# Strided attention products one place sooner, and one local mask moved behind two normalisations, in a fused attention and MLP kernel

## The chip, the cores and the metric

The kernel runs on one core of a Trainium2 chip. The metric is the device time of one execution in microseconds (us); lower is better. A core has five engines that run their own instruction streams side by side and wait for one another by semaphores: TensorE (PE, matrix products and transposes, results in PSUM), VectorE (DVE), ScalarE (ACT), GpSimd (POOL) and SyncE (SP, which starts transfers). Each engine takes its instructions in the order in which the program emits them, so in this kernel, whose schedule is written by hand, the place of a line in a list decides what an engine does first.

## The reference

Sparse attention over 8 images of 576 tokens with 8 heads of 64, and an MLP with a Mish activation behind it.

```python
def _attn_ref(q, k, v):                      # (8, 8, 576, 64) each
    scores = (1 / sqrt(D)) * q @ k.transpose(0, 1, 3, 2)
    rel = pos[:, None] - pos[None, :]
    mask_local   = (rel >= 0) & (rel < 32)                       # heads 0..3
    mask_strided = (rel >= 0) & (pos[None, :] % 32 == pos[:, None] % 32)   # heads 4..7
    attn = softmax(where(mask, scores, -1e9))
    return attn @ v

def _moe_ref(x, w_in, w_out):                # x (4608, 512): tokens x (heads, dim)
    h = x @ w_in                             # (4608, 2048)
    g = h * tanh(softplus(h))                # Mish
    return g @ w_out                         # (4608, 512)
```

## The kernel before

The 4608 tokens are cut into nine blocks of 512. Stage t of the main loop does the MLP of block t: first MLP1 (`w_in`, then Mish on ACT), then MLP2 (`w_out`). Both are lists of small groups of matmuls. Between the groups, stage t also computes the attention of image t + 1, one step of a list at each place, so that PE always has matmuls of the MLP to do while other engines work on the attention.

The main loop, cut. `g1` are the groups of MLP1, `a1` the steps put between them; `at` are the steps put between the groups of MLP2. For t = 3 to 6 the lists are `str_steps` and `loc_steps`:

```python
for t in range(NBLK):
    x, y, z = accs
    # ... (stages 0 to 2 use other lists)
    elif t + 1 < B:
        a1 = str_steps(t + 1)
        at = loc_steps(t + 1, x, y)
    # ...
    for i, g in enumerate(g1):
        g()
        if i < len(a1):
            for s in a1[i]:
                s()
    # ... casts and loads for later images
    for i, g in enumerate(mlp2(t, gT, out_accs, fc_major=(t == 0))):
        g()
        if i < len(at):
            for s in at[i]:
                s()
```

A group of MLP2 is four matmuls of 512 columns. The first six groups of MLP1 are four matmuls each, too, and so are the ten behind them (more and shorter ones where a block wraps around the end of its buffer, as in t = 4).

The two lists that the change touches:

```python
def str_steps(b):
    a = Attn(b)
    V = lambda i: (lambda: a.pv("s", i))
    return [
        [], [], [V(0)], [V(1)], [V(2)], [V(3)], [V(4)], [V(5)], [V(6)], [V(7), a.xt_str],
    ]

def loc_steps(b, x, y):
    a = Attn(b)
    Q = lambda i_acc, *parts: (lambda: a.qk(parts, i_acc))      # scores on PE, exp on ACT
    M = lambda kd, i: (lambda: a.mask(kd, i, nc.vector))
    V = lambda i: (lambda: a.pv("l", i))
    more = b + 1 < B
    n2 = (("n", 2),) if more else ()
    N = [lambda i=i: a.mask("n", i, nc.gpsimd) for i in range(3)]
    return [
        [],
        [Q(x, ("l", 0)), Q(None, ("l", 2), *n2), Q(y, ("l", 1)), M("l", 0), M("l", 2)],
        [], [],
        [V(0), V(1), M("l", 1)],
        [V(5)] + ([Q(x, ("n", 0)), Q(y, ("n", 1))] + N) * more + [a.xt_str_copy],
        [V(2)],
        [V(3)],
        [V(4), lambda: a.xt_loc(0, NW)],
        [], [], [], [], [], [], [],
    ]
```

"s" is strided, "l" local, "n" the strided scores of the next image. The local probabilities of six query tiles lie in three buffers: part 0 serves tiles 0 and 1 (and half of 2), part 1 the rest of 2, and 3 and 4, part 2 tile 5. A mask multiplies one such part by zeros and ones; a `pv` step multiplies the masked probabilities by v on PE and divides by the sum on DVE:

```python
def mask(self, kind, i, meng):
    # pm: a part of the probabilities, two halves x tiles x columns; mk: the mask, broadcast
    meng.tensor_tensor(out=pm, in0=pm, in1=mk..., op=ALU.mult)

def pv(self, kind, i):
    po = tile_t("po")...                     # one of two PSUM buffers
    self.pv_mm(kind, i, po)                  # four products on PE
    nc.vector.reciprocal(rden[0:m, :], po[0:m, :, D])
    nc.vector.tensor_tensor(out=dst..., in0=po[0:m, :, 0:D], in1=rden..., op=ALU.mult)

def xt_str(self):                            # twelve transposes on DVE, behind V(7)
    for q in range(4):
        for m in range(0, 96, 32):
            nc.vector.transpose(xs_t[32*q:32*q+32, :, :, m:m+32], src[m:m+32, :, :, q, :])

def xt_str_copy(self):                       # their result into the MLP's input, on ACT
    for c in range(2):
        nc.scalar.copy(...)
```

Of the kernel before, what the change touches and what calls it, by code (L numbers as in the profile page):

```python
# [38 lines left out]
def kernel(ctx, tc, q, k, v, moe_w_in, moe_w_out, out):  # L39
# [368 lines left out]
    def str_steps(b):  # L408

        a = Attn(b)  # L410
        V = lambda i: (lambda: a.pv("s", i))
        return [
            [], [], [V(0)], [V(1)], [V(2)], [V(3)], [V(4)], [V(5)], [V(6)], [V(7), a.xt_str],
        ]

    def loc_steps(b, x, y):

        a = Attn(b)
        Q = lambda i_acc, *parts: (lambda: a.qk(parts, i_acc))
# [4 lines that stand above are left out]
        N = [lambda i=i: a.mask("n", i, nc.gpsimd) for i in range(3)]  # L424
        return [
            [],
            [Q(x, ("l", 0)), Q(None, ("l", 2), *n2), Q(y, ("l", 1)), M("l", 0), M("l", 2)],
            [], [],
            [V(0), V(1), M("l", 1)],
            [V(5)] + ([Q(x, ("n", 0)), Q(y, ("n", 1))] + N) * more + [a.xt_str_copy],  # L430
            [V(2)],
            [V(3)],
            [V(4), lambda: a.xt_loc(0, NW)],
            [], [], [], [], [], [], [],
        ]
# [131 lines left out]
    with tc.manual_schedule():  # L567
# [35 lines left out]
        a = Attn(0)  # L603
# [69 lines left out]
        for t in range(NBLK):  # L673
            x, y, z = accs
# [3 lines left out]
            if t == 0:  # L678
                ts, at = t_steps(1), attn_steps(1, y, y)
                at[0] = ts[2:4] + [cast_v1]  # L680
                at[9] += [lambda: str_by_dma(2), lambda: loc_by_dma(2)]
                out_accs, accs = (z, x), (y, z, x)
            else:
                if t <= 2:
                    at = attn_steps(t + 1, x, y, z if t == 2 else None)
# [3 lines that stand above are left out]
                if t == 1:  # L689
                    at[9].append(lambda: str_by_dma(3))  # L690
                if t == 2:
                    Dv.memset(x_s[64:96], 0.0)
                if t + 2 < B:
                    at[9].append(lambda: loc_by_dma(t + 2))
                if 1 < t < B - 3:
                    at[9].append(lambda: str_by_dma(t + 3))
                out_accs, accs = (z, y), (z, x, y)
# [61 lines left out]
```

The softmax here doesn't subtract the row's maximum and nothing guards it: scores larger than these inputs give would overflow.

## Time and profile before

| | |
|---|---|
| time, median of 3 runs | 314.95 us (314.67 to 316.58) |
| profiled span | 312.8 us, 5771 instructions |
| PE busy | 295.3 us (94%) |
| ACT busy | 182.6 us (58%) |
| DVE busy | 164.6 us (53%) |
| POOL busy | 102.4 us (33%) |

Times inside the profile are counted from the start of the span. A line of the timeline gives the start, the length, the engine, the line of the program, the operation, the operands with their shapes, the number of instructions merged into the line, and in brackets how long the engine stood idle before it and what ended that. The chain that ended last is followed back from the last instruction; its shares tell which engine the end of the kernel hangs on. A table of windows gives, for each stretch, its length and then the busy time of each engine with its number of instructions, the granted clock of PE, the busy share of the DMA engines, and GB/s. PE's ends are modelled, so its starts are the safer numbers.

### The profile page before, as it was taken

How to read it: one execution, taken by the hardware profiler on the slowest of the kernel's cores; microseconds unless marked ns; L12 is line 12 of the kernel's file. 1: busy time of each engine (PE TensorE's matmuls, PEld its weight loads, DVE VectorE, ACT ScalarE, POOL GpSimd, SP SyncE). 2: the span in 40 equal slices, each digit the busy share in tenths (PEclk: the TensorE clock that was granted, in tenths of full speed). 3: DMA queues.
4: the chain of work that ended last, by engine and by line, in shares of the span. 5: the costliest groups of instructions: out<-in, count | busy, mean ns of one | idle time of the engine just before them, and what ended most of it. 6: DMA issues, size and time to landing. Idle time of an engine off the chain costs nothing.

```text
span 312.8 us, 5771 instructions
## 1 busy us (share of the span) xinstructions
PE 295.3 (94%) x2376; PEld 156.2 (50%) x2376; DVE 164.6 (53%) x378; ACT 182.6 (58%) x195; POOL 102.4 (33%) x109
## 2 busy tenths in 40 slices
PE   0687999999999999999999999999999999999995
PEld 0563455544454445554469754545454444444444
DVE  7673066700571048569786988698869870000000
ACT  1673653476647673867786778677767937215501
POOL 9199043263046105230791079108800000000000
PEclk9999999999999999999999999999999999999999
DMA  6999999999999999999987999898330030011011
GB/s 174 203 226 206 221 185 199 176 168 130 222 188 207 126 221 187 197 165 211 188 162 127 208 169 185 146 198 159 103 107 2 0 132 4 0 67 69 0 67 67
DMA packets 96985, 45.14 MB, mean 144 GB/s; under 512 B 79040, under 2 KB 89600, under 8 KB 96960
## 3 DMA queue, kind: packets, MB, share of 16 engines
q1 hardware_dynamic: 85520, 35.66, 61.8%
q0 software_dynamic: 11152, 8.92, 18.8%
q8 instruction: 18, 0.29, 0.4%
q10 hardware_dynamic: 288, 0.21, 0.2%
q14 instruction: 7, 0.06, 0.1%
HBM read 36.78 MB, written 9.44 MB: 148 GB/s over the span
## 4 chain that ended last, share of the span: by engine, by line
PE 85%; DVE 11%; ACT 2%; issue 1%; DVEq 0%
PE psh L507 38%; PE pso L530 31%; PE po L323 5%; PE pso L557 4%; PE ps L286 3%; DVE xs_t L397 3%; DVE Pl L307 2%; DVE ks L149 1%; DVE x_l L335 1%; PE trx L362 1%; PE tr L209 1%; DVE x_s L335 1%; PE trx L372 1%; DVE rden L334 1%; DVE Ps L601 0%
## 5 line engine op out<-in xcount | busy, mean ns | idle before, releaser
L507 PE MATMUL psh<-xT,w_in 128*128 128x512 bf16 (+1 forms) x640 | 131.9, 361 | 0.3 <-ACT Ps L299 0.3
L530 PE MATMUL pso<-w_out,gT 128*128 128x512 bf16 x512 | 121.8, 379 | 0.0
L513 ACT ACTIVATE gT<-psh 128x1024 bf16<-128x1024 f32 x72 | 72.4, 1023 | 50.1 <-PE psh L507 50.1
L507 PEld LDWEIGHTS <-w_in 128*128 128x128 bf16 x640 | 60.5, 98 | 57.1 <-issue 2.5
L530 PEld LDWEIGHTS <-gT 128*128 128x128 bf16 x512 | 45.4, 98 | 45.8
L149 POOL CAST kl<-kl 96x768 bf16<-96x768 f32 (+1 forms) x13 | 12.5, 984 | 78.8 <-DMA kl<-in_k_dram 78.8
L397 DVE STREAM_TRANSPOSE xs_t<-x_s 32x512 bf16<-32x512 bf16 x48 | 33.7, 702 | 0.9
L334 DVE RECIPROCAL rden<-po 72x4 f32<-72x4 f32 (+1 forms) x100 | 17.6, 176 | 28.1 <-PE po L323 27.2
L537 ACT COPY osb<-pso 128x1024 f32<-128x1024 f32 x16 | 17.6, 1100 | 24.3 <-PE pso L530 13.9
L307 DVE TENSOR_TENSOR Ps<-Ps,consts_sb 72x864 bf16<-72x864 bf16 (+3 forms) x15 | 10.2, 688 | 38.6 <-ACT Ps L299 38.6
L149 DVE COPY osb<-pso 128x512 f32<-128x512 f32 (+1 forms) x2 | 1.1, 558 | 51.3 <-PE pso L557 51.3
L388 DVE STREAM_TRANSPOSE xT<-x_l 32x384 bf16<-32x384 bf16 x48 | 27.3, 569 | 0.7
L149 POOL CAST vl<-vl 128x768 bf16<-128x768 f32 (+2 forms) x30 | 23.6, 785 | 9.0 <-DMA vl<-in_v_dram 7.6
L299 ACT ACTIVATE Ps<-ps 72x864 bf16<-72x864 f32 (+3 forms) x21 | 17.4, 860 | 13.4 <-PE ps L286 13.4
L335 DVE TENSOR_TENSOR x_s<-po,rden 72x256 bf16<-72x256 f32 x56 | 23.5, 420 | 1.9
L323 PEld LDWEIGHTS <-Ps 72*128 72x128 bf16 x256 | 15.5, 101 | 12.0 <-DVE Ps L307 0.8
L404 ACT COPY xT<-xs_t 128x576 bf16<-128x576 bf16 x8 | 21.4, 2938 | 0.0
L299 ACT ACTIVATE Pl<-ps 128x960 bf16<-128x960 f32 (+1 forms) x20 | 17.3, 874 | 3.7 <-PE ps L286 3.5
L335 DVE TENSOR_TENSOR x_l<-po,rden 96x256 bf16<-96x256 f32 x44 | 18.5, 421 | 1.5
L323 PE MATMUL po<-vs,Ps 72*128 72x65 bf16 x256 | 18.2, 201 | 0.7 <-DVE x_s L349 0.5
L147 ACT COPY xT<-trx 128x576 bf16<-128x576 bf16 x16 | 9.9, 636 | 14.7 <-PE trx L372 11.5
L149 POOL CAST ql<-ql 96x768 bf16<-96x768 f32 (+1 forms) x13 | 12.2, 965 | 8.7 <-DMA ql<-in_q_dram 8.7
(73 smaller groups left out, 224.3 us busy)
## 6 DMA issues: line engine op xcount, KB each, us to landing
out_dram<-osb SPq DMA_DIRECT2D x16, 512.0 KB, 4.9
vs<-in_v_dram SPq DMA_DIRECT2D x8, 576.0 KB
vl<-in_v_dram SPq DMA_DIRECT2D x8, 576.0 KB, 11.2
kl<-in_k_dram SPq DMA_DIRECT2D x7, 576.0 KB, 17.0
ql<-in_q_dram SPq DMA_DIRECT2D x7, 576.0 KB, 10.8
w_out<-in_moe_w_out_dram POOLq DMA_DIRECT2D x4, 512.0 KB, 14.2
ks<-in_k_dram POOLq DMA_DIRECT2D x7, 288.0 KB, 8.0
qs<-in_q_dram POOLq DMA_DIRECT2D x7, 288.0 KB, 8.8
```

The source lines that it names most:

```text
L149: eng.tensor_copy(out_, in_)
L299: nc.scalar.activation(pt[0:n, :, 0:nw], t[0:n, :, o0:o0 + nw], AF.Exp, scale=scale)
L323: nc.tensor.matmul(po[:, h, :], lhsT=pt[0:n, c0:c0 + 128], rhs=rhs, start=True, stop=True,)
L334: nc.vector.reciprocal(rden[0:m, :], po[0:m, :, D])
L335: nc.vector.tensor_tensor(out=dst.rearrange("p (h d) -> p h d", h=4), in0=po[0:m, :, 0:D], in1=rden[0:m, :].unsqueeze(2).to_broadcast([m, ...
L388: nc.vector.transpose(dst[32 * q:32 * q + 32, :, :, m:m + 32], src[m:m + 32, :, :, q, :])
L397: nc.vector.transpose(xs_t[32 * q:32 * q + 32, :, :, m:m + 32], src[m:m + 32, :, :, q, :])
L404: nc.scalar.copy(xT[:, 2 + c, t0:t0 + S].rearrange("p (n j) -> p j n", j=CS), xs_t[:, :, c, 0:PN])
L507: nc.tensor.matmul(ps[:, u, o:o + n], lhsT=w_in[:, cc, fc * 128:(fc + 1) * 128], rhs=xT[:, cc, a:a + n], start=(cc == 2 and o == 0), stop= ...
L513: nc.scalar.activation(gT[:, 2 * g:2 * g + 2, :], ps[:], AF.Mish)
L530: nc.tensor.matmul(p[:, ot % 2, :], lhsT=gT[:, fc, 128 * ot:128 * ot + 128], rhs=w_out[:, fc, :], start=(fc == 0), stop=(fc == 15),)
L537: nc.scalar.copy(osb[:], p[:])
```

## The change

Two edits, both to the order of steps in stages 3 to 6. The strided products of an image come one place sooner among the groups of MLP1, so that the twelve transposes on DVE behind the last of them are over sooner and DVE is free for the local masks when MLP2 begins. And the mask of the third local part, which only tile 5 needs, is no longer done right behind the first mask but behind the normalisations of tiles 0 and 1, so that these need not wait for it.

```diff
@@ str_steps
         return [
-            [], [], [V(0)], [V(1)], [V(2)], [V(3)], [V(4)], [V(5)], [V(6)], [V(7), a.xt_str],
+            [], [V(0)], [V(1)], [V(2)], [V(3)], [V(4)], [V(5)], [V(6)], [V(7), a.xt_str],
         ]
@@ loc_steps
             [],
-            [Q(x, ("l", 0)), Q(None, ("l", 2), *n2), Q(y, ("l", 1)), M("l", 0), M("l", 2)],
+            [Q(x, ("l", 0)), Q(None, ("l", 2), *n2), Q(y, ("l", 1)), M("l", 0)],
             [], [],
-            [V(0), V(1), M("l", 1)],
+            [V(0), V(1), M("l", 2), M("l", 1)],
             [V(5)] + ([Q(x, ("n", 0)), Q(y, ("n", 1))] + N) * more + [a.xt_str_copy],
```

No instruction is added or taken away. Every engine runs the same instructions on the same data; only PE's and DVE's orders differ.

## The prediction

> **What bounds the kernel now.** I read the page first. TensorE (PE) is busy for 295.3 of 312.8 us and is 85% of the chain that ended last; the only other engine with weight there is VectorE (DVE), with 11%.
>
> ```profile
> PE 295.3 (94%) x2376; PEld 156.2 (50%) x2376; DVE 164.6 (53%) x378; ACT 182.6 (58%) x195; POOL 102.4 (33%) x109
> ...
> PE 85%; DVE 11%; ACT 2%; issue 1%; DVEq 0%
> ```
>
> So the time is the PE stream plus the holes that DVE tears into it. Next I cut the span where the changed lines run. The two edited lists are used by four stages only (token blocks t = 3 to 6, which compute images 4 to 7). The windows by stage, from the first MLP1 matmul of one block to that of the next:
>
> ```profile
> 129.60:161.68 32.08, 31.42 (x246) 15.40 (x243) 25.13 (x56) 22.72 (x23) 14.54 (x14) 1.00 1.14 181
> 161.68:192.93 31.25, 31.18 (x305) 21.42 (x304) 25.49 (x56) 22.32 (x22) 14.64 (x15) 1.00 0.94 170
> 192.93:224.05 31.12, 31.03 (x241) 15.23 (x240) 25.45 (x56) 22.30 (x22) 15.46 (x15) 1.00 0.80 151
> 224.05:254.21 30.16, 30.16 (x209) 14.62 (x208) 24.87 (x56) 20.06 (x18) 1.65 (x2) 1.00 0.24 69
> ```
>
> First number: length; second: PE busy. Nearly every microsecond is PE work: there is little to win in these stages, and much room to lose. Last, the order of time around the first local products. In stage t=3, DVE first and PE below it:
>
> ```profile
> 140.59 8.58 DVE L397 STREAM_TRANSPOSE xs_t<-x_s 32x512 bf16<-32x512 bf16 x12
> 149.20 1.58 DVE L307 TENSOR_TENSOR Pl<-Pl,consts_sb 128x960 bf16<-128x960 bf16 x2
> 150.91 0.18 DVE L334 RECIPROCAL rden<-po 96x4 f32<-96x4 f32 x1
> 151.12 0.42 DVE L335 TENSOR_TENSOR x_l<-po,rden 96x256 bf16<-96x256 f32 x1
> 151.46 0.17 DVE L334 RECIPROCAL rden<-po 96x4 f32<-96x4 f32 x1
> 151.67 0.42 DVE L335 TENSOR_TENSOR x_l<-po,rden 96x256 bf16<-96x256 f32 x1
> 152.01 0.65 DVE L307 TENSOR_TENSOR Pl<-Pl,consts_sb 128x960 bf16<-128x960 bf16 x1
> ```
> ```profile
> 147.41 2.76 PE L530 MATMUL pso<-w_out,gT 128*128 128x512 bf16 x12
> 150.57 0.43 PE L323 MATMUL po<-vl,Pl 128*128 128x65 bf16 x8 [0.40 <-DVE Pl L307]
> 150.84 1.02 PE L530 MATMUL pso<-w_out,gT 128*128 128x512 bf16 x4
> 151.70 0.29 PE L323 MATMUL po<-vl,Pl 128*128 128x65 bf16 x4
> ```
>
> DVE: twelve transposes, masks l0 and l2 together (the 1.58), then reciprocal and multiplication for local tile 0, the same for tile 1, then mask l1. PE: twelve MLP2 matmuls, the eight products of tiles 0 and 1 (they need mask l0), four MLP2 matmuls, then the four products of tile 5, which need mask l2. Times are starts; a group's own end is modelled and overlaps the next, so I work from starts. When nothing holds PE, the eight products start 2.60 us after the twelve matmuls (181.59 against 178.99 in t=4), tile 5 follows the eight by 1.13 (151.70-150.57) and the reciprocal of tile 0 follows them by 0.34 (150.91-150.57).
>
> What PE loses now at the eight products is their start less (start of the twelve + 2.60): t=3 150.57-150.01 = 0.56; t=4 0.00; t=5 212.94-212.69 = 0.25; t=6 243.77-243.73 = 0.04. Sum 0.85 us. At tile 5 only t=4 loses: 182.94-181.59 = 1.35, so 0.22. **All there is to win is 0.85+0.22 = 1.07 us, 0.34% of the span.**
>
> **What the Trainium skill says.** "TensorE: Matmul & The Clock Gate", table at the top and section "What overlaps and what doesn't" in Part 3: weight loads can be pulled ahead, matmuls run strictly in order. The trace agrees: in t=3 the MLP2 matmuls behind the eight products start only after them, although their operands were ready. So a product that waits for a mask holds all of MLP2. "VectorE: DVE Perf Modes", "The perf-mode tier table" and "The TRN2 errata": a bf16 multiplication of two tensors does two elements per cycle at 0.96 GHz, with a fixed part that the page fits as 151 cycles. As an estimate that is (192+151)/0.96 = 357 ns for mask l2 (384 elements) and 657 ns for l0 and l1 (960); undisturbed ones in the trace take 0.35 (t=6) and 0.66. "GPSIMD Engine Reference", "Specifications": GpSimd shares SBUF interfaces with VectorE and collides with instructions of two SBUF inputs, as masks are. The trace agrees: l0 of t=3 runs 1.31 us where GpSimd casts k from 148.41 for 1.59, l2 of t=4 runs 0.98 within the cast from 180.87, l0 of t=5 0.94. In each, the mask ends its undisturbed length after about the end of the cast that was running.
>
> **The change, part by part.** It removes and adds no instruction. The order of instructions on ACT, GpSimd and the DMA queues is the same; only PE and DVE are reordered.
>
> *Part 1: strided products one place sooner.* One place in MLP1 is four matmuls and four products: 139.60-138.61 = 0.99 us. The last strided normalisation, hence the twelve transposes (8.58 us back to back), begin and end 0.99 sooner. Mask l0 then is bound by the exp on ACT that writes its input, which starts at 147.44, 179.02, 210.12, 241.23 and takes 0.97 (ends 148.41, 179.99, 211.09, 242.20; I add 0.04 for the semaphore). New start of l0: t=3 148.45 instead of 149.20; t=4 180.03 instead of 180.79; t=5 211.13 instead of 211.94; t=6 242.24 instead of 243.06. So 0.75 to 0.82 sooner. Its end: in t=3 and t=5 the first of two k casts is just running (148.41+0.8, 210.78+0.8), so l0 ends at about 149.8 and 212.1; in t=4 and t=6 it is free and ends at 180.7 and 242.9. All are before the times at which PE arrives (150.01, 181.59, 212.69, 243.73). **Part 1 wins the whole 0.85.** Nothing else waits for the earlier products: strided tile 0 now comes after 8 matmuls of MLP1, 1.73 us into the stage, its result 0.3 us later, and DVE has ended the previous local transposes by then (158.66+4.66 = 163.32 against 161.68+1.73+0.3 = 163.7 in t=4); its v cast has ended too (162.2 on GpSimd).
>
> *Part 2: mask l2 behind the first two normalisations.* Before, l2 stood in the 0.34 us in which DVE waited for the first product anyway: in t=3, 5 and 6 the reciprocal came at its natural 0.34, so l2 cost nothing there. Now it starts after two normalisations. Reciprocal to reciprocal is 0.55 (151.46-150.91), so l2 starts 0.34+2x0.55 = 1.44 after the eight products, takes 0.35, and PE starts about 0.06 after a mask's end (mask l0 of t=3: 149.20+1.31 = 150.51, products 150.57). Tile 5 comes at 1.44+0.35+0.06 = 1.85 after the eight, where PE is there at 1.13: **a new hole of 0.72 us in each of the four stages**, in place of one of 0.22 in one stage. In t=5, l2 would start at 212.69+1.44 = 214.13, inside the first q cast of GpSimd (213.91 to about 214.7): add 0.45, hole 1.17-ish instead of 0.72. In t=3 (q cast at 151.72, l2 at 151.45), t=4 (k cast over at 183.02, l2 at 183.03) and t=6 (no casts) it is free.
>
> *Sum by stage,* start of tile 5 after against before: t=3 150.01+1.85 = 151.86 against 151.70, +0.16; t=4 181.59+1.85 = 183.44 against 182.94, +0.50; t=5 212.69+1.85+0.45 = 214.99 against 214.07, +0.92; t=6 243.73+1.85 = 245.58 against 244.91, +0.67. Total +2.25. Everything behind tile 5 keeps its distance to it: mask l1 ends by about 0.65 (or 1.4 behind a cast) after l2, and tile 2, which needs it, comes 1.66 after tile 5 (153.36-151.70); the next strided scores go through PE and ACT behind tile 5 as before. Since stages without this edit do not change, 314.95+2.25 is 317.2; I write 317.1, as the cast collision of t=5 depends on when a transfer lands.
>
> **The rivals.** *A: part 1 alone decides, and l2 hides.* Then the kernel gains 0.85 to 1.07: 313.9 to 314.1. For it: l0's wait is the one that the profile names at PE. Against: only 0.86 us of MLP2 matmuls lie between tile 1's products and tile 5's, and DVE needs 1.45 for two normalisations and the mask. *B: both cancel*, if DVE begins the first normalisation sooner than I count or l2's cost is nearly that of the old wait: about 315. Against: 0.34 is seen in all of t=3, 5 and 6. *C: a larger loss.* Mask l1 now follows l2 directly and ends later, so tile 2 can wait as well where casts take turns with masks (t=5: l2 to 214.94, then a cast, l1 near 216.3 against tile 2 at 216.65). If this or the copies of ACT slip over their margins (an exp of the next scores ends at 154.27, MLP2's third tile, which takes that PSUM, starts at 154.48), another 0.5 us per stage: 318 to 319. The margins are small, but both sides hang on the same tile 5, so they should move together.
>
> **Range and chances.** The sum of four holes with 0.15 to 0.25 of doubt each, 0.5 for the collision in t=5, and the spread of the times before (314.67 to 316.58) give 315.9 to 318.3. Two per cent is 6.3 us: the gain is capped at 1.07 and the loss would need three times my sum. Faster 0.01, same 0.97, slower 0.02.
>
> **What would show it.** Right: in each of the four stages the eight products start 2.60 after their twelve matmuls, DVE sits idle before the first local reciprocal, and PE waits at tile 5's products for DVE's mask, 1.85 after the eight. Part 1 is wrong if l0 still ends after PE's arrival; part 2 is wrong if tile 5 follows the eight by less than 1.4; the step "keeps its distance" is wrong if tile 2 follows tile 5 by more than 1.66 or the stages grow by more than tile 5 is late. A time under 315 would mean that l2 hides.

## The result, and the profile after

The changed kernel takes 317.6 us (median of 6 runs, 316.77 to 318.26) against 315.53 us for the kernel before (median of 6 runs, three of them those of the table before): ratio 1.0065, 95% interval 1.004 to 1.009. It is 2.1 us slower. The profiled execution has a span of 315.6 us.

From the page of the changed kernel, the busy time of each engine:

```profile
PE 293.0 (93%) x2339; PEld 156.2 (49%) x2376; DVE 163.6 (52%) x378; ACT 182.9 (58%) x195; POOL 103.2 (33%) x109
```

The work is the same; PE's busy sum is lower only because 37 matmul records are missing from this trace (2339 against 2376). The windows by stage (length first, then PE's busy time), cut at the same places as before (within 0.2 us of the first MLP1 matmul of each block):

```profile
130.07:162.29 32.22, 31.04 (x241) 15.42 (x243) 23.74 (x54) 22.73 (x23) 15.35 (x15) 1.00 1.10 185
162.29:194.33 32.04, 31.02 (x302) 21.44 (x304) 26.17 (x56) 22.35 (x22) 16.61 (x17) 1.00 0.97 167
194.33:226.20 31.87, 30.55 (x237) 15.25 (x240) 25.88 (x56) 22.32 (x22) 13.75 (x13) 1.00 0.79 148
226.20:257.03 30.83, 30.07 (x205) 14.60 (x208) 24.95 (x56) 20.05 (x18) 1.66 (x2) 1.00 0.24 67
```

Against the windows before, the four stages are longer by 0.14, 0.79, 0.75 and 0.67 us, 2.35 in all. By the starts of the first MLP1 matmuls of t=3 and t=7 themselves, the four stages take 124.40 us before (129.65 to 254.05) and 126.75 after (130.12 to 256.87), again 2.35 more. The first stage also begins 0.47 later than before (130.07 against 129.60). No instruction before that point was changed, so this is the spread of single executions, and the two spans (315.6 and 312.8) differ by more than the medians do.

The order of time in stage t=3, DVE first:

```profile
148.91 0.66 DVE L307 TENSOR_TENSOR Pl<-Pl,consts_sb 128x960 bf16<-128x960 bf16 x1
150.80 0.18 DVE L334 RECIPROCAL rden<-po 96x4 f32<-96x4 f32 x1 [1.23 <-PE po L323]
151.01 0.42 DVE L335 TENSOR_TENSOR x_l<-po,rden 96x256 bf16<-96x256 f32 x1
151.35 0.17 DVE L334 RECIPROCAL rden<-po 96x4 f32<-96x4 f32 x1
151.56 0.42 DVE L335 TENSOR_TENSOR x_l<-po,rden 96x256 bf16<-96x256 f32 x1
151.90 0.91 DVE L307 TENSOR_TENSOR Pl<-Pl,consts_sb 128x384 bf16<-128x384 bf16 x2
```

and PE beside it:

```profile
147.87 2.76 PE L530 MATMUL pso<-w_out,gT 128*128 128x512 bf16 x11
150.47 0.42 PE L323 MATMUL po<-vl,Pl 128*128 128x65 bf16 x8
150.73 1.02 PE L530 MATMUL pso<-w_out,gT 128*128 128x512 bf16 x4
152.30 0.30 PE L323 MATMUL po<-vl,Pl 128*128 128x65 bf16 x4 [0.54 <-DVE Pl L307]
```

The first mask is done at 149.57, 0.90 us before PE comes to the eight products of tiles 0 and 1 (150.47, which is 2.60 after the twelve matmuls). DVE then stands idle for 1.23 us: the slot in which the third mask used to be done at no cost. The third mask now comes only after both normalisations, at 151.90, and PE, which has reached tile 5 at 150.47 + 1.13 = 151.60, starts it at 152.30. The largest entry of what PE waits for in the four stages (total, number of waits, longest):

```profile
PE po L323 <- DVE Pl L307: 2.8, 4, 0.9
```

Four waits, one per stage, all on a mask of DVE. The wait at the eight products has gone, and a larger one stands at tile 5.

### The profile page after: what moved, and what is told of

It reads as the page before. It is cut to its first block, busy times and chain, and to the rows that moved or that the text cites. A ratio compares the mean times of both kernels' runs of the same rounds, so it can differ in the third digit from the quotient of the medians.

```text
span 315.6 us, 5734 instructions
## 1 busy us (share of the span) xinstructions
PE 293.0 (93%) x2339; PEld 156.2 (49%) x2376; DVE 163.6 (52%) x378; ACT 182.9 (58%) x195; POOL 103.2 (33%) x109
## 4 chain that ended last, share of the span: by engine, by line
PE 87%; DVE 9%; issue 2%; ACT 1%
PE psh L507 39%; PE pso L530 32%; PE po L323 5%; PE pso L557 4%; PE ps L286 3%; DVE x_l L335 2%; DVE ks L149 1%; DVE Pl L307 1%; DVE rden L334 1%; PE trx L362 1%; DVE x_s L335 1%; PE tr L209 1%; PE trx L372 1%; DVE x_s L349 0%; DVE Ps L601 0%
## 5 line engine op out<-in xcount | busy, mean ns | idle before, releaser
L530 PE MATMUL pso<-w_out,gT 128*128 128x512 bf16 x487 | 117.9, 379 | 2.1 <-issue 1.0
L149 POOL CAST kl<-kl 96x768 bf16<-96x768 f32 (+1 forms) x13 | 13.6, 1067 | 79.8 <-DMA kl<-in_k_dram 79.8
L307 DVE TENSOR_TENSOR Ps<-Ps,consts_sb 72x864 bf16<-72x864 bf16 (+3 forms) x15 | 8.5, 565 | 40.3 <-ACT Ps L299 40.3
L323 PE MATMUL po<-vl,Pl 128*128 128x65 bf16 x192 | 12.9, 201 | 3.8 <-DVE Pl L307 3.4
```

Source lines behind the costliest of these rows:

```text
L149: eng.tensor_copy(out_, in_)
L323: nc.tensor.matmul(po[:, h, :], lhsT=pt[0:n, c0:c0 + 128], rhs=rhs, start=True, stop=True,)
L530: nc.tensor.matmul(p[:, ot % 2, :], lhsT=gT[:, fc, 128 * ot:128 * ot + 128], rhs=w_out[:, fc, :], start=(fc == 0), stop=(fc == 15),)
```

## The experiments

All were timed beside the kernel before; ratios are to that. The number to watch in their profiles is the distance from the start of the eight products to the start of tile 5's: 1.13 us where nothing holds PE. The theory was that the mask queued behind two normalisations makes the loss and the sooner strided products only gain; the rivals were that the sooner products cost (1), that the second mask, pushed behind the third, does it (2), and that GpSimd's casts do it (3).

**The strided products alone.**

```diff
 # str_steps as changed; loc_steps as before
+            [], [V(0)], [V(1)], ... [V(6)], [V(7), a.xt_str],
             [Q(x, ("l", 0)), ..., M("l", 0), M("l", 2)],
```

> Only the strided products one place sooner; the third local mask stays behind the first. Theory (the loss comes from the third mask queued behind two normalisations, the sooner strided products only gain): no wait at tiles 0 and 1 and none at tile 5, so 1.07 us faster than before the change (0.85 + 0.22), ratio about 0.9966; tile 5 starts 1.13 us after the eight products in all four stages. Rival 1 (the sooner strided products themselves cost, because they meet DVE's local transposes at the start of a stage): slower than before by most of the 2.1 us of the whole change.

Measured: 313.93 us against 315.09, ratio 0.9976 (0.9961 to 0.9992). Faster, by 0.8 us as a ratio and 1.2 by the medians. The timeline of DVE in its stage t=4, the two masks in one line first:

```profile
179.42 1.55 DVE L307 TENSOR_TENSOR Pl<-Pl,consts_sb 128x960 bf16<-128x960 bf16 x2
181.31 0.18 DVE L334 RECIPROCAL rden<-po 96x4 f32<-96x4 f32 x1 [0.34 <-PE po L323]
```

and of PE there:

```profile
180.99 0.42 PE L323 MATMUL po<-vl,Pl 128*128 128x65 bf16 x8
182.11 0.29 PE L323 MATMUL po<-vl,Pl 128*128 128x65 bf16 x4
```

Both masks are over by 180.97, just before PE arrives at 180.99, although a cast stretches them to 1.55; the reciprocal still follows the products by 0.32, and tile 5 by 1.12. In t=3 casts stretch them to 2.11, so that the reciprocal comes 0.46 after the products, and tile 5 still at 1.14. In the four stages the distance is 1.14, 1.12, 1.12 and 1.12, and the eight products start with no wait. Rival 1 falls.

**The mask alone.**

```diff
 # str_steps as before; loc_steps as changed
-            [Q(x, ("l", 0)), ..., M("l", 0), M("l", 2)],
+            [Q(x, ("l", 0)), ..., M("l", 0)],
-            [V(0), V(1), M("l", 1)],
+            [V(0), V(1), M("l", 2), M("l", 1)],
```

> Only the third local mask behind the two normalisations; the strided products stay where they were. Theory: the waits at tiles 0 and 1 stay (0.85 us) and tile 5 comes 1.85 us after the eight products, or 2.15 where a GpSimd cast runs into the mask: 0.72 + 0.50 + 0.72 + 0.71 = 2.65 us slower than before, up to 3.2 with collisions in two stages, ratio 1.0085 to 1.010; slower than the whole change by 0.4 to 1. Rival 1 (the strided products cost): no slower than before by more than 0.5.

Measured: 318.31 us against 315.09, ratio 1.0118 (1.0096 to 1.0141): 3.2 us slower by the medians, 3.7 by the ratio. The distances are 2.15, 2.08, 2.17 and 1.84; GpSimd casts met the third mask in three stages, not two. So this edit alone costs more than the whole change, and the other one takes some of that back: about 1 us by the medians, 1.4 to 1.7 by the ratios. The cost is above what was expected (2.65 to 3.2), and the trace shows a wait that no expectation had, 0.56 us of a strided product in t=4 for GpSimd's cast of v:

```profile
165.85 0.28 PE L323 MATMUL po<-vs,Ps 72*128 72x65 bf16 x4 [0.56 <-POOL vs L149]
```

GpSimd was late there because a q cast ahead of it had waited for its load until 156.09 (151.72 before); that the edit brings this about is not shown. And one part of the expectation failed: the waits at the eight products did not stay at 0.85. In its stage t=3:

```profile
149.74 0.66 DVE L307 TENSOR_TENSOR Pl<-Pl,consts_sb 128x960 bf16<-128x960 bf16 x1
```

The strided products are late here as they were before, yet the first mask takes 0.66 (1.31 before, under a cast), and the eight products start at 150.54 with no wait. In the four stages the waits there are 0, 0.08, 0.19 and 0.03, 0.30 in all. The 0.56 us that PE lost in t=3 before was thus not the late transposes alone, but the transposes and a cast that came just then.

**The mask between the two normalisations.**

```diff
-            [V(0), V(1), M("l", 2), M("l", 1)],
+            [V(0), M("l", 2), V(1), M("l", 1)],
```

> The whole change, but the third mask between the normalisations of tiles 0 and 1 instead of behind both. Theory: the mask starts 0.34 + 0.55 = 0.89 us after the eight products, ends at 1.24, tile 5 at 1.30 where PE is there at 1.13: four holes of 0.17, 0.7 in all against a gain of 1.07, so 0.4 us faster than before (equal, at worst, with casts in the way). Rival 2 (it is the second mask, pushed behind the third, and tile 2 or the normalisation of tile 5 that wait for it): that mask ends when it did in the changed kernel, so as slow as that, 2 us over before.

Measured: 314.94 us against 315.09, ratio 1.0005 (0.9988 to 1.0022): no different from before. DVE in its stage t=3:

```profile
150.90 0.18 DVE L334 RECIPROCAL rden<-po 96x4 f32<-96x4 f32 x1 [1.24 <-PE po L323]
151.45 0.34 DVE L307 TENSOR_TENSOR Pl<-Pl,consts_sb 128x384 bf16<-128x384 bf16 x1
151.72 0.17 DVE L334 RECIPROCAL rden<-po 96x4 f32<-96x4 f32 x1
152.27 0.65 DVE L307 TENSOR_TENSOR Pl<-Pl,consts_sb 128x960 bf16<-128x960 bf16 x1
```

and PE:

```profile
150.57 0.42 PE L323 MATMUL po<-vl,Pl 128*128 128x65 bf16 x8
151.85 0.30 PE L323 MATMUL po<-vl,Pl 128*128 128x65 bf16 x4
```

The mask starts 0.88 after the products and tile 5 comes at 1.28 (1.28, 1.29, 1.29 in the others; 1.30 was expected). The second mask starts 1.70 after the products, as late as it would behind both normalisations and the third mask (1.44 + 0.27), and harms nothing: rival 2 falls. By its times the kernel can't be told from the one before; the expected 0.4 us lies at the edge of the interval. Its profile says more. The four stages take 124.00 us against 124.40, so they gain the 0.40 that was expected, and this execution lost 0.83 us elsewhere, in stage t=1, which no edit touches:

```profile
79.81 0.57 PE L286 MATMUL ps<-qTs,kTs 64*128 64x72 bf16 x24 [0.83 <-DMA qTs<-qs]
```

**Tile 5 one place later.**

```diff
-            [V(5)] + ([Q(x, ("n", 0)), Q(y, ("n", 1))] + N) * more + [a.xt_str_copy],
-            [V(2)],
+            ([Q(x, ("n", 0)), Q(y, ("n", 1))] + N) * more + [a.xt_str_copy],
+            [V(5)],
+            [V(2)],                      # and tiles 3 and 4 one place later each
```

> The whole change, but the products of tile 5, and with them tiles 2, 3 and 4, come one place (four MLP2 matmuls) later; the next image's strided scores stay at their place. Theory: only the distance counts. Tile 5 then comes naturally about 2.7 us after the eight products (2.1 in the last stage), later than the mask at 1.85 to 2.15, so no hole is left and the gain of the first part stays: 0.9 to 1.1 us faster than before. Rival 2, or a cost at the stage's end (local transposes on DVE reach 1 us further into the next stage): 1 us or more slower than before.

Measured: 314.05 us against 315.09, ratio 0.9968 (0.9955 to 0.9982). That is 1.0 us faster than before, as expected. The mask is as late as in the changed kernel, but it is done when PE comes to tile 5. PE in the stage t=3:

```profile
149.59 0.42 PE L323 MATMUL po<-vl,Pl 128*128 128x65 bf16 x8
152.24 0.29 PE L323 MATMUL po<-vl,Pl 128*128 128x65 bf16 x4
```

The distance is 2.65 (2.66, 2.65 and 1.99 in the others) and contains no wait for the mask. So a late mask does not cost anything by itself; it costs where its reader stands too near behind it. This kernel and the one with the strided products alone are both faster than the kernel before; between the two there is no difference to be seen.

**GpSimd's casts out of the way,** with the changed kernel run again beside it.

```diff
 # stages 3 to 5: casts of the next k and q behind the three strided masks of GpSimd
-                cast_qk_loc(t + 2, Po, Po)        # ahead of MLP2
+                at[5] += [cast_qk_loc, cast_v]    # behind the step that holds N
```

> The whole change, with GpSimd's casts of the next k and q (stages 3 to 5) put behind its three strided masks, so that no cast runs while VectorE does the local masks. Theory: the wait at tile 5 has a fixed part, two normalisations and the mask, and a part that comes only where a q cast is running when the third mask begins (0.30 us in two of the stages of the changed kernel, t=4 and 5). Without casts tile 5 starts 1.83 to 1.85 us after the eight products in all four stages, and the kernel is 0.6 us faster than the changed one, still 1.5 us slower than before. Rival 3 (the casts are the cause, the queue on VectorE is not): the distance falls to 1.13 and the loss is gone, 1 us faster than before. If something later waits for the casts, the time goes up and a wait shows elsewhere.

> The changed kernel once more, beside the one with the casts moved, on the same chip. Theory: 2.1 us (0.65%) slower than before, tile 5 at 1.83 after the eight products where no cast runs into the third mask, 2.1 to 2.2 where one does. Rival 3: where no cast runs into it, 1.13.

Measured: 318.86 us (ratio 1.0117, 1.0095 to 1.0139) with the casts moved, 317.25 (1.0073, 1.0051 to 1.0095) for the changed kernel, against 314.98. With the casts moved the distance is 1.83 in all four stages, so rival 3 falls, and the fixed part is what I took it for: 0.70 of hole in each stage with no cast near. In the changed kernel's second profile the distances are 1.83, 2.40, 1.83 and 1.83: one stage was hit this time, two in the first. That stage, t=4, in the timeline of GpSimd,

```profile
184.63 2.30 POOL L149 CAST ql<-ql 96x768 bf16<-96x768 f32 x2 [0.93 <-DMA ql<-in_q_dram]
```

of DVE,

```profile
184.76 1.48 DVE L307 TENSOR_TENSOR Pl<-Pl,consts_sb 128x384 bf16<-128x384 bf16 x2
```

and of PE:

```profile
183.33 0.42 PE L323 MATMUL po<-vl,Pl 128*128 128x65 bf16 x8
185.73 0.30 PE L323 MATMUL po<-vl,Pl 128*128 128x65 bf16 x4 [1.11 <-DVE Pl L307]
```

The q cast starts when its transfer lands, 0.13 before the third mask here, and the mask, 0.35 by itself, lets PE go only at 185.73. But the kernel with the casts moved is not 0.6 faster than the changed one; it is 1.6 slower. Its waits name a new one:

```profile
PE ps L286 <- DMA qTs<-qs: 1.7, 2, 1.0
```

In two stages (t=3 and 4) PE now waits for the transposes, made by transfers, of the strided q of the next image; these 1.7 us are about what the kernel is slower by. The chain shows why: these transposes (L170) are issued on SyncE behind the local ones (L178), which need the casts that now come later.

```profile
159.54 1.54 POOL kl L149 x2
161.08 1.54 POOL ql L149 x2
...
167.69 0.30 SPq L178
168.08 1.38 SPq L170
169.55 11.18 DMA qTs<-qs
```

**The four stages alone.** The times above hold whatever else an execution met. From the first MLP1 matmul of t=3 to that of t=7, one execution of each kernel shows:

| kernel | from, to | length | against before | expected |
|---|---|---|---|---|
| before | 129.65, 254.05 | 124.40 | | |
| changed | 130.12, 256.87 | 126.75 | +2.35 | +2.25 |
| changed, again | 131.26, 257.95 | 126.69 | +2.29 | +2.1 |
| strided products alone | 129.60, 252.89 | 123.29 | -1.11 | -1.07 |
| mask alone | 130.19, 258.28 | 128.09 | +3.69 | +2.65 to +3.2 |
| mask between | 130.22, 254.22 | 124.00 | -0.40 | -0.4 |
| tile 5 later | 129.24, 252.49 | 123.25 | -1.15 | -0.9 to -1.1 |
| casts moved | 129.62, 257.98 | 128.36 | +3.96 | +1.5 |

The two rows that miss are the two with a wait outside the theory: 0.56 us for the cast of v, and 1.7 us for transfers. With the casts moved, four holes of 0.70 less the 1.07 gained, and these 1.7, make 3.4; the 0.5 us left over is not explained.

## Why the prediction was right

The prediction was 317.1 us on a base of 314.95, a loss of 2.15; measured are 317.6 on a base of 315.53, a loss of 2.1. The mechanism is the one predicted, and the sizes hold in sum; in two of its terms the agreement is in part luck. By its steps:

**The natural distances** (2.60 to the eight products, 0.34 to the reciprocal, 1.13 to tile 5) held: 2.60 in t=3, 4 and 6 of the changed kernel (in t=5 the first of the twelve matmuls has no record), 0.32 to 0.33 to the reciprocal in all four, and 1.12 to 1.14 in all stages of the first experiment.

**Part 1.** The first mask starts 0.03 after its exp in all four stages (in t=3 the exp runs from 147.91 for 0.97, the mask starts at 148.91) and is done before PE comes. The gain was put at 0.85 for the wait at the eight products and 0.22 for the one at tile 5; alone, the part gave 0.8 to 1.2. The prediction names the casts that stretched the first mask in that profile, but took the waits as fixed. Without the casts the mask, 0.66 long, would have been done at 149.86 in t=3 and 212.60 in t=5, and PE, 0.06 later, would have started at its natural 150.01 and 212.69. So 0.81 of the 0.85 needed a cast beside the late transposes, and the mask-alone kernel, with transposes as late, lost only 0.30 there. A wait read from one profile has such luck in it.

**Part 2.** Tile 5 was predicted 1.85 after the eight products. It comes at 1.83 and 1.82 in t=3 and t=6, and at 2.15 and 2.12 in t=4 and t=5, where a cast runs into the mask. The collision was foreseen for t=5 alone at 0.45; it came in two stages at 0.3 each, and in the second profile in one at 0.57. So the sum by stage was right in total and not in each:

| stage | tile 5 later, predicted | tile 5 later in its stage, measured | stage longer, measured |
|---|---|---|---|
| t=3 | 0.16 | 0.13 | 0.14 |
| t=4 | 0.50 | 0.80 | 0.79 |
| t=5 | 0.92 | 0.74 | 0.75 |
| t=6 | 0.67 | 0.65 | 0.67 |
| sum | 2.25 | 2.32 | 2.35 |

**Everything behind tile 5 keeps its distance.** Tile 2 follows it by 1.67 in t=3 (153.97 - 152.30), against 1.66 before, and by 1.67 in t=4 and t=5 (186.02 - 184.35, 217.88 - 216.21); in t=6, where no strided scores stand between, by 1.01 against 0.99. The stages grow by what tile 5 is late, to within 0.02. So the margins held, and rival C (more is lost behind it) didn't come about. Rival A (the third mask hides) is false for the change but true for its first half alone. Rival B (both cancel) is near to what the mask between the two normalisations gives: with a hole of 0.15 instead of 0.70 per stage, the four stages gain 0.40, and the times of the whole kernel show no difference.

## What to carry to other kernels

Before moving an instruction back on an engine that runs in order, look at what that engine does at the old place: if it waits there anyway, the instruction is free, and moving it buys nothing. Then count, at the new place, the work in front of it against what its reader's engine has left to do; if the reader's engine is the bound, the difference is paid in full, at every repetition. An edit that has two halves is worth timing as halves: here one half gains about 1 us, the other loses 3 or more, and the sum hides both.

## What the runs showed of the hardware

Masks on DVE and casts on GpSimd delayed one another in these traces. In the changed kernel's second profile, t=4, the first of the two q casts runs from 184.63 for 0.83 us. The third mask starts inside it, at 184.76, and ends at 185.67, 0.21 after the cast: 0.91 us instead of the 0.35 that it takes with no cast near. The second cast starts at 185.42, while this mask is still running, and takes 1.51 instead of 0.82. The delay lies inside the length that the profile reports, not in a gap before it. In all profiles, masks of 0.66 us took up to 1.31, masks of 0.35 up to 0.98, and pairs of casts, 1.59 undisturbed, up to 2.40. Which masks are hit depends on when a load lands, and differed between executions of one kernel (two stages in one profile of the changed kernel, one in the other). With the casts moved away, no mask took more than 0.66 in the four stages. The prediction had expected a collision at one fixed place.
